# Joining a 64-bit weight's sign and low bits by half-word passes in an attention and gated feed-forward kernel

## The chip, the cores and the metric

The kernel runs on one core of one Trainium2 chip, as one program. The metric is device microseconds of one execution. Each number of the result is a median over runs, with the lowest and highest beside it. The engines have short names: PE multiplies matrices, DVE works on vectors, ACT applies functions and scales, POOL works across partitions and issues some DMAs, SP issues most DMAs. ACT issues DMAs too, the weight loads among them.

## The reference

Attention over 8 batches of 8 heads, 576 positions, head size 64, with a causal mask and a bias from a running sum of `s`; then, for the 4608 tokens of width 512, a gated layer of width 1536.

```python
scores = scale * np.matmul(q, k.transpose(0, 1, 3, 2))
s_pos = np.maximum(s, 0.0)
cum = np.cumsum(s_pos, axis=-1)
bias = -(cum[:, :, :, None] - cum[:, :, None, :])
scores = np.where(causal, -1000000000.0, scores + np.minimum(bias, 0.0))
scores = scores - np.max(scores, axis=-1, keepdims=True)
attn = np.exp(scores)
attn = attn / (np.sum(attn, axis=-1, keepdims=True) + 1e-09)
attn_out = np.matmul(attn, v)
x = attn_out.transpose(0, 2, 1, 3).reshape(B * S, H * D)
gate = 1.0 / (1.0 + np.exp(-(x @ w_gate)))
val = x @ w_val
out = (gate * val @ w_out).astype(np.float32)
```

`q`, `k`, `v` and `s` come in 32-bit floats. The three weight matrices come in 64-bit floats, and the kernel turns them into 32-bit floats itself.

## The kernel before

**Heads.** Attention goes head by head, each in five tiles of query rows (64 rows, then four of 128). The program is written as a sequence of ticks, five to a head. The first 8 heads (one batch) run in 32-bit floats: scores on PE (`n_s`, L575), masked and reduced to a row minimum of the negated scores on DVE (`n_max`, L584), the exponential on ACT (L587), a transpose on PE (L596) copied out by ACT (L597), the product with `v` on PE (`n_av`, L605). A score bank is given back to PE when DVE has reduced it. Later heads use high and low 16-bit parts and transposing DMAs (`s_part`, `max_part` with L471, `p_part`, `av_part`).

**Weights.** They come in 18 steps (`wsteps`): 12 for the columns of `w_gate` and `w_val`, 128 at a time, and 6 for the rows of `w_out`, 256 at a time. A step holds 1024 weights in each of the 128 partitions. `load_weight` (L253 to L260) brings them as pairs of 32-bit words, low word first, into a raw buffer: `ws`, parts of `w2all`, or parts of `t2f`. `decode_weight` makes a 32-bit float from each pair in the buffer `a` (the names `wa`, or a part of `w2all`). `split_weight` sums the squares on ACT (L287), adds them up across the partitions on POOL (L289), makes a power-of-two scale on DVE (L125, L127), and writes a high and a low 16-bit part (ACT L292, DVE L293). The raw buffers are few, so the load of a later step waits until an earlier one has been decoded.

**The decode.** A 64-bit float has its sign, an 11-bit exponent and the first 20 bits of the fraction in the high word. ACT (L272) reads the high word as a 32-bit float and multiplies it by 2^-112, which shifts the exponent's range so that 3 bits to the left it is that of a 32-bit float. Then three DVE passes work on the result: L273 shifts left by 3 and clears the sign into a buffer `m`, L274 puts the sign bit back from `a`, and L275 adds the three top bits of the low word, shifted right by 29. L273 has one tensor operand, L274 and L275 have two.

**Order.** Engines run their own lists in order. The lists are made when the kernel is built, by a scheduler that follows the written order, priorities (`first`) and its own estimate of time; so a change to one pass can change the order of instructions on every engine. Up to tick 44 the weight steps are called at fixed ticks, later a few ahead of the feed-forward units that use them. Feed-forward units (`ffn_in` with L657, `ffn_out` with L687) begin at tick 44 and fill PE between attention pieces.

Of the kernel before, what the change touches and what calls it, by code (L numbers as in the profile page):

```python
# [7 lines left out]
F16 = mybir.dt.float16  # L8
F32 = mybir.dt.float32
F32R = mybir.dt.float32r  # L10
I32 = mybir.dt.int32
I64 = mybir.dt.int64
AF = mybir.ActivationFunctionType
ALU = mybir.AluOpType
# [9 lines left out]
def tile_attention_then_gated_ffn(  # L24
# [11 lines left out]
    nc = tc.nc  # L36
# [33 lines left out]
    w1 = [cp.tile([P, NC, 2, 2, P], F16, name=f"w1_{f}") for f in range(NF)]  # L70

    w2all = cp.tile([P, NF // 2, 2, 8, 2, DM // 8], F16, name="w2all")
# [49 lines left out]
    def pow2_of(dst, ss, tag):  # L122

        e = wp.tile([P, 1], I32, tag="xe", name=f"xe_{tag}")
        nc.vector.tensor_scalar(e, ss.bitcast(I32), 1, 0x3F800000, ALU.logical_shift_right, ALU.bitwise_and)  # L125
        n = dst.shape[1]
        nc.vector.tensor_scalar(dst.bitcast(I32), e.to_broadcast([P, n]) if n > 1 else e, -1.0, 204.0 * 2.0 ** 23,  # L127
                                ALU.mult, ALU.add)

    def inverse_pow2(dst, sc):  # L130
        nc.vector.tensor_scalar(dst.bitcast(I32), sc.bitcast(I32), -1.0, 254.0 * 2.0 ** 23, ALU.mult, ALU.add)

# [79 lines left out]

    raw0 = lp.tile([P, 8 * P, 2], I32, name="ws0")
    dec0 = lp.tile([P, 8 * P], I32, name="wa0")
    flat = w2all.rearrange("p f l h x n -> p (f l h x n)").bitcast(I32)
# [11 lines left out]
    def room(n):  # L227

        o, f = wsteps[n]
        if o == 0:  # L230
            return raw[f % 3], dec[f % 3], n - 3
        i, j, last = outroom[f // 2]
        return raw[i], dec[j], last
# [30 lines left out]
    def decode_weight(n):  # L264

        o, f = wsteps[n]
        r, a, _ = room(n)
        if not wide:
            return a.bitcast(F32)
        m = w2all[:, f // 2].rearrange("p l h x n -> p (l h x n)") if o else w1[f].rearrange("p c g l n -> p (c g l n)")  # L270
        m = m.bitcast(I32)
        nc.scalar.activation(a.bitcast(F32), r[:, :, 1].bitcast(F32), AF.Copy, scale=2.0 ** -112)  # L272
        nc.vector.tensor_scalar(m, a, 3, 0x7FFFFFF8, ALU.logical_shift_left, ALU.bitwise_and)  # L273
        nc.vector.scalar_tensor_tensor(a, a, -0x80000000, m, ALU.bitwise_and, ALU.bitwise_or)  # L274
        nc.vector.scalar_tensor_tensor(a, r[:, :, 0], 29, a, ALU.logical_shift_right, ALU.bitwise_or)  # L275
        return a.bitcast(F32)

    def split_weight(n, a):
# [41 lines left out]
    def weight_step():  # L320
        n = wnext["step"]
        while n and wnext["load"] < len(wsteps) and room(wnext["load"])[2] < n:
            if not NF <= wnext["load"] < NF + 2:
                load_weight(wnext["load"])
            wnext["load"] += 1
        split_weight(n, decode_weight(n))
        wnext["step"] = n + 1
# [413 lines left out]
    for n in range(nticks + 12):  # L741
# [13 lines left out]
        if 2 <= n < nticks + 2:  # L755
            a, z = divmod(n - 2, NTL)
# [5 lines left out]
        if 1 <= n < nticks + 1:  # L762
            a, z = divmod(n - 1, NTL)
# [7 lines left out]
        if 3 <= n < 3 + NTL * NN:  # L771
            with first():
                a, z = divmod(n - 3, NTL)
# [11 lines left out]
        if i < NH:  # L785
            p, j = divmod(i, 2)
            b, h = divmod(i, H)
# [79 lines left out]
            elif b == 1:  # L867
                if VSQ <= n < VSQ + vch:
                    v_square(2, n - VSQ)
                if VSQ + 5 <= n < VSQ + 5 + vch:  # L870
                    c = VSQ + 4 + vch - n
# [15 lines left out]
        if n >= NE and state["u"] < 2 * NF:  # L887
            fdone = min(NF, int((n - NE + 1) * FPT))
            while state["u"] < 2 * fdone:
                f = state["u"]  # L890
# [17 lines left out]
        m = n - (11 if n > 2 * NTL * H + 30 else 7)  # L908
        b = m // (NTL * H) if m >= 0 else 0
        if b >= 1:  # L910
            r = m - b * NTL * H + 1
# [39 lines left out]
```

## Time and profile before

| what | value |
|---|---|
| median of 3 runs | 1152.38 us (1151.87 to 1155.03) |
| profiled execution, span from first to last instruction | 1146.4 us |
| what lies around the span, by that median | 6.0 us |
| mean granted TensorE clock | 0.985 of full speed |
| PE, DVE, ACT, POOL busy, share of the span | 95%, 68%, 65%, 23% |
| DMA queue of SP and ACT (q1), share of 16 engines | 57.6% |
| first feed-forward matrix product (L657) | 119.2 us |
| decode passes on DVE, first and last start | 11.5 us and 175.2 us |

The profiled execution's own time outside its span is not listed, so the 6.0 us is the difference of the median and the span. Busy shares are averages over stages with different limits: an engine that is at 68% of the whole may be full in one stage. Where a row names a line, the tile names follow as output, arrow, inputs, with buffer numbers left out; a wait is given with the engine and line whose end came last.

### The profile page before, as it was taken

How to read it: one execution, taken by the hardware profiler on the slowest of the kernel's cores; microseconds unless marked ns; L12 is line 12 of the kernel's file. 1: busy time of each engine (PE TensorE's matmuls, PEld its weight loads, DVE VectorE, ACT ScalarE, POOL GpSimd, SP SyncE). 2: the span in 40 equal slices, each digit the busy share in tenths (PEclk: the TensorE clock that was granted, in tenths of full speed). 3: DMA queues.
4: the chain of work that ended last, by engine and by line, in shares of the span. 5: the costliest groups of instructions: out<-in, count | busy, mean ns of one | idle time of the engine just before them, and what ended most of it. 6: DMA issues, size and time to landing. Idle time of an engine off the chain costs nothing.

```text
span 1146.4 us, 30336 instructions
## 1 busy us (share of the span) xinstructions
PE 1091.6 (95%) x11644; PEld 853.5 (74%) x11644; DVE 776.1 (68%) x2395; ACT 749.5 (65%) x1465; POOL 261.3 (23%) x568
## 2 busy tenths in 40 slices
PE   6787888989999999999999999999999999999998
PEld 4566676658767887788777777778877887787775
DVE  6899999866787777776565677777777775222222
ACT  6989778667777777676665577767776764233222
POOL 6634233222232222121211122212222221000000
PEclk9889899999999999999999999999999999999999
DMA  9676868995989888777646498868887774000000
GB/s 280 201 217 161 185 139 181 183 189 130 171 164 175 164 178 167 141 150 138 145 79 139 89 178 166 166 144 171 156 161 138 150 124 88 13 20 20 1 19 19
DMA packets 445518, 157.62 MB, mean 137 GB/s; under 512 B 403583, under 2 KB 435839, under 8 KB 445374
## 3 DMA queue, kind: packets, MB, share of 16 engines
q1 hardware_dynamic: 418686, 127.38, 57.6%
q10 hardware_dynamic: 23328, 17.04, 4.9%
q0 software_dynamic: 3360, 11.27, 3.0%
q8 instruction: 91, 1.49, 0.5%
q14 instruction: 53, 0.43, 0.1%
HBM read 56.92 MB, written 9.58 MB: 58 GB/s over the span
## 4 chain that ended last, share of the span: by engine, by line
PE 76%; DMA 7%; DVE 5%; issue 5%; ACT 5%; SPq 1%; POOL 1%; ACTq 0%; DVEq 0%; POOLq 0%
PE gv L657 42%; PE o L687 22%; PE s L447 3%; PE s L446 3%; DMA qk<-in_q_dram 1%; PE av L506 1%; PE av L508 1%; PE av L507 1%; DMA v<-in_v_dram 1%; DVE e L471 1%; PE s L575 1%; DMA pt<-p 1%; DMA T<-T 1%; PE na_ps L605 1%; DMA nqk<-in_q_dram 1%
## 5 line engine op out<-in xcount | busy, mean ns | idle before, releaser
L657 PE MATMUL gv<-x,w 128*128 128x256 f16 (+3 forms) x6912 | 613.2, 246 | 5.3 <-DVE t2f L664 2.7
L657 PEld LDWEIGHTS <-w 128*128 128x128 f16 x6912 | 533.8, 98 | 61.5 <-issue 5.2
L687 PE MATMUL o<-w2all,h 128*128 128x512 f16 x1296 | 314.8, 379 | 0.0
L461 POOL TENSOR_SCALAR_AFFINE_SELECT rl<-rl 128x64 f32<-128x64 f32 (+1 forms) x280 | 111.5, 399 | 519.7 <-DVE em L471 465.3
L474 ACT ACTIVATE e<-e,em 128x576 f32<-128x576 f32 x280 | 154.6, 554 | 92.3 <-DVE em L471 90.2
L687 PEld LDWEIGHTS <-h 128*128 128x128 f16 x1296 | 123.6, 98 | 108.7 <-issue 2.4
L662 ACT ACTIVATE th<-gv,scb 128x256 f32<-128x256 f32 (+3 forms) x288 | 111.4, 412 | 139.3 <-PE gv L657 138.4
L664 DVE SCALAR_TENSOR_TENSOR t<-th,gv 128x256 f32<-128x256 f32 x192 | 80.2, 417 | 133.5 <-ACT th L662 132.5
L471 DVE CUSTOM_DVE_ANT_0 e<-s,rl,qkcf 128x288 f32<-128x288 f32 x280 | 135.8, 485 | 30.5 <-PE s L447 24.9
L672 ACT ACTIVATE h<-t,hsc 128x256 f16<-128x256 f32 x192 | 96.6, 503 | 80.0 <-DVE t L664 80.0
L483 DVE SCALAR_TENSOR_TENSOR p<-e,p 128x384 f16<-128x384 f32 x224 | 102.0, 495 | 40.2 <-ACT p L478 39.4
L673 DVE SCALAR_TENSOR_TENSOR h<-t,hsc,h 128x256 f16<-128x256 f32 x192 | 93.2, 486 | 43.3 <-ACT h L672 42.8
L478 ACT ACTIVATE p<-e 128x1152 f16<-128x1152 f32 x112 | 112.1, 1001 | 2.8
L506 PE MATMUL av<-v,pt 128*128 128x65 f16 x560 | 68.0, 193 | 6.9 <-DMA pt<-p 6.9
L507 PE MATMUL av<-v,pt 128*128 128x64 f16 x560 | 68.0, 192 | 0.0
L446 PE MATMUL s<-T 128*128 128x288 f16 (+2 forms) x246 | 64.6, 280 | 3.6 <-DMA T<-qk 2.6
L508 PE MATMUL av<-v,pt 128*128 128x65 f16 x560 | 67.9, 194 | 0.0
L447 PE MATMUL s<-T 128*128 128x288 f16 (+2 forms) x246 | 62.2, 282 | 2.4 <-DMA T<-T 2.4
L506 PEld LDWEIGHTS <-pt 128*128 128x128 f16 x560 | 52.4, 97 | 13.6 <-DMA pt<-p 8.8
L706 POOL DMA_DIRECT2D out_dram<-osb x34 | 19.4, 570 | 174.6 <-ACT osb L705 173.8
L409 POOL PARTITION_BROADCAST cr<-cr x63 | 57.5, 913 | 6.1 <-DVE em L584 5.7
L455 DVE TENSOR_SCALAR rl<-cr,qkcf 128x576 f32<-128x576 f32 x56 | 29.1, 520 | 40.1 <-POOL cr L409 39.9
(157 smaller groups left out, 1436.9 us busy)
## 6 DMA issues: line engine op xcount, KB each, us to landing
v<-v SPq DMA_DIRECT2D x56, 162.5 KB
out_dram<-osb POOLq DMA_DIRECT2D x34, 256.0 KB, 2.9
v<-in_v_dram SPq DMA_DIRECT2D x64, 128.0 KB
T<-T SPq DMA_DIRECT2D x82, 72.0 KB
t2f<-in_v_dram SPq DMA_DIRECT2D x20, 288.0 KB
qk<-in_q_dram SPq DMA_DIRECT2D x17, 288.0 KB
qk<-in_k_dram SPq DMA_DIRECT2D x17, 288.0 KB
w2all<-in_moe_w_gate_dram ACTq DMA_DIRECT2D x7, 512.0 KB
```

The lines of the kernel that those rows point to most:

```text
L446: nc.tensor.matmul(ps[:, : b_ - a], lhs, T[i][:, 0, a:b_], start=True, stop=False)
L447: nc.tensor.matmul(ps[:, : b_ - a], lhs, T[i][:, 2, a:b_], start=False, stop=True)
L461: nc.gpsimd.affine_select(rl[i][:, q0:w], rl[i][:, q0:w], pattern=[[-1, m]], compare_op=ALU.is_ge, fill=-MASKED if i < NN else MASKED, bas ...
L471: nc.vector.tensor_tensor_reduce(e_t[t][:, a:b_], ps[:, : b_ - a], rl[i][:, a:b_], c, init, ALU.add, ALU.min, acc)
L474: nc.scalar.activation(e_t[t][:, :w], e_t[t][:, :w], AF.Exp, bias=init, scale=-1.0)
L478: nc.scalar.activation(p_s[h_][:, 0], e_s[h_], AF.Copy, scale=PSCALE)
L483: nc.vector.scalar_tensor_tensor(flat[:, LOW[t] * P : (LOW[t] + t) * P], e_t[t][:, : t * P], PSCALE, flat[:, kb * P : (kb + t) * P], ALU.m ...
L506: nc.tensor.matmul(AV[i][:, t], hi, v_[:, D : 2 * D + 1], start=kb == 0, stop=False)
L657: nc.tensor.matmul(ps[:, gv, a:e], w1[f][:, cc, gv, wl], x_of(b, cc)[:, xl, c0 + a : c0 + e], start=(c == 0), stop=(c == 3 * NC - 1))
L662: nc.scalar.activation(th[:, a:e], ps[:, 0, a:e], AF.Tanh, scale=scb[b][:, f : f + 1])
L672: nc.scalar.activation(h[:, 0], t2, AF.Copy, scale=hsc[:, f : f + 1])
L687: nc.tensor.matmul(ps[:m], h[:, hl, tt * P : tt * P + m], w2[f][:, wl], start=(f == 0 and c == 0), stop=(f == NF - 1 and c == 2))
```

## The change

The decode keeps ACT's scaling and has one merging pass instead of two. Two passes with one operand work on the loaded words as 16-bit halves (half 0 and 1 are the low word, 2 and 3 the high word). The first puts the top three bits of half 1 into half 0; the second puts the sign bit of half 3 into half 1. The low word then holds the sign at its top, the three bits at its bottom and zeros between. The one merging pass shifts ACT's result left by 3, which drops its sign, and joins it with that word. The buffer `m` isn't used any more.

```diff
+I16 = mybir.dt.int16
...
         if not wide:
             return a.bitcast(F32)
-        m = w2all[:, f // 2].rearrange("p l h x n -> p (l h x n)") if o else w1[f].rearrange("p c g l n -> p (c g l n)")
-        m = m.bitcast(I32)
+        half = r.bitcast(I16)
+        nc.vector.tensor_scalar(half[:, :, 0], half[:, :, 1], 13, 7, ALU.logical_shift_right, ALU.bitwise_and)
+        nc.vector.tensor_scalar(half[:, :, 1], half[:, :, 3], -0x8000, None, ALU.bitwise_and)
         nc.scalar.activation(a.bitcast(F32), r[:, :, 1].bitcast(F32), AF.Copy, scale=2.0 ** -112)
-        nc.vector.tensor_scalar(m, a, 3, 0x7FFFFFF8, ALU.logical_shift_left, ALU.bitwise_and)
-        nc.vector.scalar_tensor_tensor(a, a, -0x80000000, m, ALU.bitwise_and, ALU.bitwise_or)
-        nc.vector.scalar_tensor_tensor(a, r[:, :, 0], 29, a, ALU.logical_shift_right, ALU.bitwise_or)
+        nc.vector.scalar_tensor_tensor(a, a, 3, r[:, :, 0], ALU.logical_shift_left, ALU.bitwise_or)
         return a.bitcast(F32)
```

In the changed kernel the two half passes are L272 and L273, ACT's scaling is L274 and the merging pass L275; other lines near them move by one. The number of instructions on DVE stays the same.

DVE's list at the first weight step, in the first head, before. In a row stand line, operation, output, arrow, inputs and size; in brackets are the engines or DMA queues whose end it awaits. ISA is the row minimum, whose name `em` carries the tile and the piece; the last number is only the buffer's.

```order
L584 ISA e_80,em_4_1_226<-s_4_288_184,cr_147,em_4_0_224 128x288 [waits DVE_49,PE_49,Pool_49]
L584 ISA em_4_1_226 128x1
L273 TENSOR_SCALAR w_0_66<-wa_137 128x1024 [waits Activation_49]
L274 SCALAR_TENSOR_TENSOR wa_137<-wa_137,w_0_66 128x1024 [waits DVE_49]
L584 ISA e_80,em_3_0_254<-s_3_0_219,cr_147 128x448 [waits PE_49,Pool_49]
L584 ISA em_3_0_254 128x1
L275 SCALAR_TENSOR_TENSOR wa_137<-ws_136,wa_137 128x1024 [waits DMAHW6_49,DMAHW5_49,DVE_49]
L584 ISA e_79,em_2_0_275<-s_2_0_244,cr_147 128x320 [waits PE_49,Pool_49]
```

And the same place in the changed kernel:

```order
L272 TENSOR_SCALAR ws_136<-ws_136 128x1024 [waits DMAHW6_49,DMAHW5_49]
L584 ISA e_80,em_4_1_226<-s_4_288_184,cr_147,em_4_0_224 128x288 [waits DVE_49,PE_49,Pool_49]
L584 ISA em_4_1_226 128x1
L273 TENSOR_SCALAR ws_136<-ws_136 128x1024 [waits DVE_49]
L275 SCALAR_TENSOR_TENSOR wa_137<-wa_137,ws_136 128x1024 [waits DVE_49,Activation_49]
L584 ISA e_80,em_3_0_254<-s_3_0_219,cr_147 128x448 [waits PE_49,Pool_49]
L584 ISA em_3_0_254 128x1
L272 TENSOR_SCALAR w2all<-w2all 128x1024 [waits DMAHW7_49,DMAHW1_49]
L584 ISA e_79,em_2_0_275<-s_2_0_244,cr_147 128x320 [waits PE_49,Pool_49]
```

The first half pass moved ahead of a row minimum and awaits the load itself; only the merging pass still awaits ACT, and the second step's first half pass stands a row minimum earlier than its L273 did.

DVE's list between the fourth head and the fifth, where the weight steps 5 to 7 stand before:

```order
L273 TENSOR_SCALAR w_6_72<-wa_137 128x1024
L275 SCALAR_TENSOR_TENSOR w2all<-w2all 128x1024
L615 TENSOR_TENSOR nx_638<-na_ps_562,ner_635 128x5x64
L632 SCALAR_TENSOR_TENSOR x_130<-nx_ps_3_524,vsc_327,x_130 128x256
L274 SCALAR_TENSOR_TENSOR wa_137<-wa_137,w_6_72 128x1024
L273 TENSOR_SCALAR w_7_73<-w2all 128x1024
L175 TENSOR_REDUCE vso_1003<-vst_1001 128x1
L275 SCALAR_TENSOR_TENSOR wa_137<-ws_136,wa_137 128x1024
L274 SCALAR_TENSOR_TENSOR w2all<-w2all,w_7_73 128x1024
L125 TENSOR_SCALAR xe_v_1007<-vso_1003 128x1
L125 TENSOR_SCALAR xe_w_1063<-wtot_1061 128x1
L584 ISA e_80,em_4_0_737<-s_4_0_711,cr_586 128x288
```

And the same place in the changed kernel:

```order
L275 SCALAR_TENSOR_TENSOR wa_137<-wa_137,ws_136 128x1024
L612 RECIPROCAL ner_635<-ner_635 128x5
L615 TENSOR_TENSOR nx_638<-na_ps_562,ner_635 128x5x64
L275 SCALAR_TENSOR_TENSOR w2all<-w2all 128x1024
L272 TENSOR_SCALAR w2all<-w2all 128x1024
L273 TENSOR_SCALAR w2all<-w2all 128x1024
L272 TENSOR_SCALAR ws_136<-ws_136 128x1024
L273 TENSOR_SCALAR ws_136<-ws_136 128x1024
L176 TENSOR_REDUCE vso_1003<-vst_1001 128x1
L584 ISA e_80,em_4_0_737<-s_4_0_711,cr_586 128x288
```

Ahead of the row minimum `em_4_0` of the next head stood four merging passes and two one-operand passes; now it is two merging passes, of steps 6 and 7, and four half passes that belong to steps 8 and 9 already, whose merging passes stand behind that minimum.

## The prediction

> **What bounds the kernel now.** First the span cut into stages, in the windows view. Each row is a stretch in us, its length, each engine's busy time, the granted TensorE clock, the share of the DMA engines and GB/s.
>
> ```profile
> core 0 of [0], span 1146.4 us
> core 0: us, PE busy (x) PEld busy (x) DVE busy (x) ACT busy (x) POOL busy (x), PEclk, DMA share, GB/s
> 10.00:60.00 50.00, 37.26 (x224) 28.12 (x223) 41.29 (x101) 46.29 (x91) 29.66 (x46) 0.88 0.82 236
> 60.00:120.00 60.00, 50.15 (x288) 39.89 (x287) 52.86 (x137) 51.18 (x95) 22.98 (x37) 0.84 0.70 188
> 120.00:180.00 60.00, 48.84 (x519) 40.54 (x517) 55.74 (x160) 45.39 (x78) 20.23 (x36) 0.97 0.84 172
> 180.00:240.00 60.00, 55.64 (x562) 42.04 (x561) 49.74 (x177) 47.92 (x95) 17.76 (x37) 1.00 0.94 179
> 240.00:1147.00 907.00, 895.26 (x10045) 699.61 (x10043) 571.02 (x1809) 555.05 (x1103) 164.34 (x385) 1.00 0.62 123
> ```
>
> From 240 us on PE is busy 895.26 of 907 us: the matrix work bounds that stretch, and nothing on DVE can shorten it. What can be won lies ahead of it. PE stands idle 12.7 us in 10 to 60 (50 less 37.26), 9.9 in 60 to 120, 11.2 in 120 to 180 and 4.4 in 180 to 240. Whatever is cut there moves the full stretch forward and shortens the run by as much. Who keeps PE waiting differs: in 10 to 60 ACT is the fullest engine (46.29 of 50, DVE 41.29), in 60 to 120 the two are level, in 120 to 180 DVE is fullest (55.74 of 60, ACT 45.39).
>
> Next the view of waits from 10 to 180 us: engine and line that waited, whom for, total us, times, the longest.
>
> ```profile
> PEld s L575 <- DVE em L584: 12.1, 14, 1.9
> ...
> PE s L575 <- DVE em L584: 7.7, 10, 1.5
> ...
> ACT w2all L287 <- DVE wa L275: 3.2, 2, 2.1
> ```
>
> PE's largest wait here is for the row minimum on DVE (L584), which frees a score bank. It is late because DVE works in order and weight passes stand ahead of it, as DVE's timeline shows:
>
> ```profile
> 74.10 1.21 DVE L274 SCALAR_TENSOR_TENSOR wa<-wa,w 128x1024 int32<-128x1024 int32 x1
> 75.23 0.68 DVE L273 TENSOR_SCALAR w<-w2all 128x1024 int32<-128x1024 int32 x1
> 75.83 0.34 DVE L584 CUSTOM_DVE_ANT_0 e<-s,cr 128x192 f32<-128x192 f32 x1
> 76.11 0.08 DVE L584 DVE_READ_ACCUMULATOR2_ANT em<- 128x1 f32 x1
> 76.11 1.21 DVE L275 SCALAR_TENSOR_TENSOR w2all<-w2all 128x1024 int32<-128x1024 int32 x1
> 77.25 1.25 DVE L275 SCALAR_TENSOR_TENSOR wa<-ws,wa 128x1024 int32<-128x1024 int32 x1
> 78.42 1.21 DVE L274 SCALAR_TENSOR_TENSOR w2all<-w2all,w 128x1024 int32<-128x1024 int32 x1
> 79.56 0.21 DVE L584 CUSTOM_DVE_ANT_0 e<-s,cr 64x64 f32<-64x64 f32 x1
> ```
>
> Between the minimum at 75.83 and the next at 79.56 stand three merging passes, 3.5 us in which PE gets no bank back. So a shorter decode does pay, though not at its full length in every stage.
>
> **The change, part by part.** The groups of DVE instructions by line and form: busy us, mean ns of one, idle before.
>
> ```profile
> L274 DVE SCALAR_TENSOR_TENSOR w2all<-w2all,w 128x1024 int32<-128x1024 int32 x8 | 10.2, 1272 | 0.0
> L275 DVE SCALAR_TENSOR_TENSOR w2all<-w2all 128x1024 int32<-128x1024 int32 x8 | 10.2, 1270 | 0.0
> ...
> L275 DVE SCALAR_TENSOR_TENSOR wa<-ws,wa 128x1024 int32<-128x1024 int32 x6 | 7.4, 1226 | 0.0
> ...
> L274 DVE SCALAR_TENSOR_TENSOR wa<-wa,w2all 128x1024 int32<-128x1024 int32 x6 | 7.3, 1212 | 0.0
> ...
> L273 DVE TENSOR_SCALAR w<-w2all 128x1024 int32<-128x1024 int32 x8 | 5.5, 693 | 2.2 <-ACT w2all L272 2.2
> ...
> L274 DVE SCALAR_TENSOR_TENSOR wa<-wa,w 128x1024 int32<-128x1024 int32 x4 | 4.9, 1217 | 0.0
> ...
> L273 DVE TENSOR_SCALAR w2all<-wa 128x1024 int32<-128x1024 int32 x6 | 4.2, 702 | 0.0
> ...
> L273 DVE TENSOR_SCALAR w<-wa 128x1024 int32<-128x1024 int32 x4 | 2.7, 680 | 0.6 <-ACT wa L272 0.5
> L125 DVE TENSOR_SCALAR xe_w<-wtot 128x1 int32<-128x1 int32 x18 | 2.6, 146 | 6.4 <-POOL wtot L289 6.3
> ...
> L141 DVE TENSOR_TENSOR_SCAN cum<-sp_sb,zero 64x576 f32<-64x576 f32 x1 | 1.3, 1349 | 0.0
> ```
>
> Removed: 18 merging passes (L274) of 1.24 us (10.2, 7.3 and 4.9 make 22.4 us, by 18) and 18 one-operand passes (L273) of 0.69 us. Added: two one-operand passes of 1024 elements for each of the 18 steps. What stays: ACT's scaling, the last merging pass, and the split into high and low parts.
>
> The **unknown** is the duration of an added pass. It reads and writes 16-bit halves, one element every 8 bytes, in place; the trace has no such instruction. The low end is L273, a one-operand pass of the same 1024 elements over 32-bit words without gaps: 0.69 us. An upper end, should such a pass go one element at a time like a merging pass, is 1.24 us. The far end is the slowest rate per element on DVE, the scan: 1349 ns less the 146 ns of an instruction with next to no elements, over 576, is 2.09 ns each, so 2.28 us for 1024 elements. I take 0.69 us. It is the nearest row, the same operation on the same count with one source and one destination in SBUF. And L275 already reads one word every 8 bytes of the loaded pairs (wa<-ws,wa, 1226 ns) at the price of L274, which reads none with gaps (1212 and 1217 ns): that gap costs a read nothing. No row shows a gapped write.
>
> [...]
>
> **The sum.** A step changes on DVE by two times 0.69 less 0.69 less 1.24, that is by -0.55 us; 18 steps by -10.0 us. Where the passes lie, in the windows view of L273 alone:
>
> ```profile
> 10.00:60.00 50.00, 5.54 (x8) 0.88 0.82 236
> 60.00:120.00 60.00, 4.19 (x6) 0.84 0.70 188
> 120.00:180.00 60.00, 2.75 (x4) 0.97 0.84 172
> ```
>
> By stage, and these fractions are my choice: in 120 to 180 DVE is the fullest engine, so 4 times 0.55 counts whole, 2.2 us. In 60 to 120 ACT is as full, so half of 6 times 0.55, 1.65 us. In 10 to 60 ACT's work covers most of it, so a quarter of 8 times 0.55, 1.1 us. Together **4.95 us**. If ACT's cover were gone, all 10.0 us would come; if it held everywhere, only the 2.2.
>
> The moved parts I cost at nothing in the sum, and at some 3 us either way in the range. The half passes no longer wait for ACT: they read the loaded words and stand in DVE's queue where the load is awaited, as the rows of the order show, so the chain behind ACT shrinks from three DVE passes to one. That takes from the 3.2 us that ACT waited for L275. The price is that DVE itself now waits for the loads, with row minima queued behind it. ACT did so in the run before:
>
> ```profile
> L272 ACT ACTIVATE w2all<-w2all 128x1024 f32<-128x1024 f32 x8 | 9.3, 1164 | 1.7 <-DMA w2all<-in_moe_w_val_dram 1.6
> ...
> L272 ACT ACTIVATE wa<-ws 128x1024 f32<-128x1024 f32 x6 | 6.9, 1145 | 1.8 <-DMA ws<-in_moe_w_val_dram 1.8
> ```
>
> The two come to 3.4 us, about what the shorter chain gives. On POOL and SP nothing is added; their weight sums and loads only follow the steps, and POOL is busy 20 to 30 us of each stretch before 180. A raw buffer is still freed by the last merging pass, so the loads are bound as before.
>
> The profiled execution has a span of 1146.4 us, and 1152.38, the median of the runs, lies 6.0 us above it; I carry those 6.0 us unchanged. 1146.4 less 4.95 is a span of 1141.5, and the time **1147.4 us**, 0.4% faster. About 0.3%, 3.5 us, is what a measurement of this kernel can tell from no change.
>
> **The rivals.**
> - *ACT and the new order eat the gain.* For it: ACT is busy 46.29 of 50 us in the first stretch, and holds the same passes as before; the loads now stop DVE. Against: DVE's 55.74 of 60 later on. Then 2.2 us, less up to 3.4 for loads, remain: between 1150.2 and 1153.6, middle 1152.
> - *One element at a time.* The half passes take 1.24 us, the change doesn't do what it says, since a shorter pass is paid twice: a step costs DVE 0.55 us more, and with the same fractions the run takes 1157.3. It decides from a pass of 0.965 us on, where two of them equal the 0.69 and 1.24 us removed. For it: 16-bit elements with gaps occur in no row; against: L273's rate on 32-bit ones.
> - *Gapped writes stall.* At the scan's rate two passes and a merge are 5.80 us where 3.17 stood, 18 times 2.63 is 47 us on DVE. Its idle time from 10 to 180 us is 20.1 us; if half of that takes some of it, 37 us are left, 1189. Same place and point of decision. [...]
>
> **How the numbers follow.** Forecast (0.69 us passes, about half of it gained) 0.43; ACT and order eat it 0.25; one element at a time 0.19; stalled writes 0.13. The forecast's own range is 1142.4 (all 10.0 us) to 1150.2. Faster by over 0.3%, below 1148.9, holds 0.41 of the forecast and 0.02 of the next: 0.43. Slower, above 1155.8, holds 0.15 of the third case, all of the fourth and 0.01 of the second: 0.29. The rest, 0.28, lies within. The range runs from 1141 to 1164: it takes in the first three cases with some 3 us for the order on each side, and leaves out most of the fourth.
>
> **What would show it.** The whole span's busy times, from the page:
>
> ```profile
> PE 1091.6 (95%) x11644; PEld 853.5 (74%) x11644; DVE 776.1 (68%) x2395; ACT 749.5 (65%) x1465; POOL 261.3 (23%) x568
> ```
>
> In the groups by line, L272 and L273 of the changed kernel at 0.69 us (step right), 1.24 (second rival) or near 2.3 (third). DVE's total should be about 10 us below 776.1, ACT's unchanged. In the windows, PE's idle time from 10 to 180 us down from 33.8 by some 5, and the stretch of full PE starting that much earlier. In the waits, L575 for L584 shorter than 7.7 us; a new wait of DVE for the weight loads would speak for the first rival. Wrong it would be if the DVE time falls and PE's idle time doesn't.

## The result and the profile after

| kernel | median us (lowest to highest) | runs |
|---|---|---|
| before | 1153.12 (1151.87 to 1155.03) | 4 |
| changed | 1186.41 (1184.95 to 1189.09) | 4 |

The changed kernel takes 1.0289 times the time of before, interval 1.027 to 1.0309: **33 us slower**, where 1147.4 us was forecast, outside the range of 1141 to 1164.

First the changed kernel's page: span, busy times by engine, and the granted TensorE clock in 40 slices.

```profile
span 1183.2 us, 30344 instructions
...
PE 1103.6 (93%) x11644; PEld 861.0 (73%) x11644; DVE 787.9 (67%) x2395; ACT 751.2 (63%) x1465; POOL 270.1 (23%) x568
...
PEclk8968789899999999999999999999999999999999
```

The span is 36.8 us longer than the 1146.4 of before. DVE is 11.8 us busier (787.9 against 776.1), where some 10 us less were forecast. PE runs the same 11644 products but is busy 12.0 us longer (1103.6 against 1091.6), and it stands idle 79.6 us of the span where it was 54.8. The 36.8 us are these two: 24.8 us more idle PE, 12.0 us more time in the same products. (By the medians it is 33.3 us: the profiled run of the changed kernel, at 1184.95 us, lies 1.75 us above its span, that of before was a quick one. So of the 6.0 us that the prediction carried around the span, some 4 were the spread between runs.)

The windows view of the changed kernel, in the same stretches; columns as before.

```profile
10.00:60.00 50.00, 36.90 (x212) 27.62 (x210) 42.78 (x94) 41.44 (x79) 30.83 (x40) 0.90 0.76 221
60.00:120.00 60.00, 37.07 (x201) 29.37 (x201) 51.71 (x114) 46.41 (x86) 28.98 (x36) 0.75 0.63 179
120.00:180.00 60.00, 44.87 (x345) 35.05 (x346) 48.18 (x131) 42.96 (x74) 19.32 (x33) 0.80 0.66 131
180.00:240.00 60.00, 51.68 (x523) 40.85 (x521) 45.67 (x165) 41.71 (x84) 15.75 (x34) 0.94 0.95 173
240.00:1184.00 944.00, 928.73 (x10354) 724.75 (x10351) 594.14 (x1884) 574.98 (x1140) 168.84 (x400) 1.00 0.62 122
```

From 240 us on PE is full in both kernels (928.73 of 944 us here). The loss lies ahead: PE is idle 22.9 us in 60 to 120 (9.9 before), 15.1 in 120 to 180 (11.2 before), and runs 201 products there where 288 ran, 345 where 519 ran. The granted clock falls too: 0.75 for 0.84 in 60 to 120, 0.80 for 0.97 in 120 to 180. Ten us at a time, the changed kernel first:

```profile
60.00:70.00 10.00, 5.08 (x22) 4.53 (x23) 7.76 (x12) 8.80 (x20) 7.90 (x9) 0.50 0.70 226
70.00:80.00 10.00, 4.76 (x30) 3.80 (x29) 8.20 (x21) 4.72 (x7) 0.60 (x2) 0.84 0.81 233
80.00:90.00 10.00, 5.31 (x16) 3.47 (x16) 9.29 (x22) 7.46 (x13) 6.16 (x8) 0.50 0.43 141
```

and the kernel before:

```profile
60.00:70.00 10.00, 10.00 (x42) 8.45 (x41) 8.36 (x21) 8.94 (x15) 3.23 (x4) 0.58 1.11 335
70.00:80.00 10.00, 7.53 (x53) 5.80 (x51) 10.00 (x21) 8.05 (x16) 4.08 (x6) 1.00 0.32 89
80.00:90.00 10.00, 7.36 (x38) 4.72 (x39) 8.13 (x29) 8.98 (x17) 3.29 (x9) 1.00 1.12 290
```

In 80 to 90 the changed kernel's PE has half its clock throughout and is busy for 5.31 us; before, it had the full clock and was busy for 7.36. No value below 0.50 stands in these rows, and a value between 0.50 and 1.00 is a mean of the two: the clock records in the traces of both kernels, and of e2 to e12 below, hold 1.00 and 0.50 alone. So the whole span's mean tells the time at half: 0.968 of 1183.2 us gives 2 times 0.032 times 1183.2, 76 us; before, 0.985 of 1146.4 gives 34 us. All runs bear out the direction, at a smaller distance: 0.960 to 0.968 in the four of the changed kernel, 0.973 to 0.985 in the seven of before that stood beside e11 and e12. The profiled run of before is at the top of its kind: the 26 runs of before beside e7 to e10 have a median clock of 0.979, which by the same sum is some 48 us at half.

The groups of DVE instructions by line and form, changed kernel: busy us, mean ns of one, idle time before and its releaser.

```profile
L273 DVE TENSOR_SCALAR w2all<-w2all 128x1024 int16<-128x1024 int16 x9 | 12.5, 1392 | 0.0
L272 DVE TENSOR_SCALAR w2all<-w2all 128x1024 int16<-128x1024 int16 x9 | 12.2, 1355 | 4.5 <-DMA w2all<-in_moe_w_val_dram 2.9 <-DMA w2all<-in_moe_w_out_dram 1.6
...
L272 DVE TENSOR_SCALAR ws<-ws 128x1024 int16<-128x1024 int16 x6 | 8.3, 1389 | 1.4 <-DMA ws<-in_moe_w_val_dram 1.4
...
L273 DVE TENSOR_SCALAR t2f<-t2f 128x1024 int16<-128x1024 int16 x3 | 4.4, 1479 | 0.0
...
L272 DVE TENSOR_SCALAR t2f<-t2f 128x1024 int16<-128x1024 int16 x3 | 4.0, 1325 | 4.3 <-DMA t2f<-in_moe_w_out_dram 4.3
```

A half pass takes 1.33 to 1.48 us by these means, not 0.69, and DVE now stands still for weight loads: 4.5, 1.4 and 4.3 make 10.2 us, where before it never did. The waits from 10 to 180 us:

```profile
PEld s L575 <- DVE em L584: 26.4, 15, 3.1
...
PE s L575 <- DVE em L584: 23.1, 14, 2.9
...
ACT e L587 <- DVE em L584: 10.3, 9, 3.6
```

PE's wait for the row minimum has grown from 7.7 to 23.1 us, its weight loads' from 12.1 to 26.4 (the two lie largely in the same gaps). DVE's timeline shows one place (start us, duration, instruction, in brackets the idle time before):

```profile
72.73 1.30 DVE L272 TENSOR_SCALAR ws<-ws 128x1024 int16<-128x1024 int16 x1 [1.18 <-DMA ws<-in_moe_w_val_dram]
74.06 1.30 DVE L273 TENSOR_SCALAR ws<-ws 128x1024 int16<-128x1024 int16 x1
75.16 0.20 DVE L176 TENSOR_REDUCE vso<-vst 128x1 f32<-128x4 f32 x1
75.20 0.45 DVE L584 CUSTOM_DVE_ANT_0 e<-s,cr 128x288 f32<-128x288 f32 x1
```

Row minima follow in DVE's list behind 1.18 us of waiting for a load and 2.6 us of half passes. Here the wait and the longer pass stand ahead of the same consumer.

### The profile page after: what moved, and what is told of

It is laid out like the page before. It is cut to its first block, busy times and chain, and to the rows that moved or that the text cites. A ratio compares the mean times of both kernels' runs of the same rounds, so it can differ in the third digit from the quotient of the medians.

```text
span 1183.2 us, 30344 instructions
## 1 busy us (share of the span) xinstructions
PE 1103.6 (93%) x11644; PEld 861.0 (73%) x11644; DVE 787.9 (67%) x2395; ACT 751.2 (63%) x1465; POOL 270.1 (23%) x568
## 4 chain that ended last, share of the span: by engine, by line
PE 69%; DMA 4%; issue 4%; DVE 3%; POOL 1%; SPq 1%; ACT 1%; DVEq 0%; POOLq 0%; ACTq 0%
PE gv L657 39%; PE o L687 21%; PE s L447 2%; PE s L446 2%; DMA v<-in_v_dram 1%; PE av L506 1%; PE av L508 1%; DMA T<-qk 1%; PE av L507 1%; DMA pt<-p 1%; DVE e L471 1%; POOL rl L461 1%; PE av L510 1%; PE av L511 1%; DVE p L483 0%
## 5 line engine op out<-in xcount | busy, mean ns | idle before, releaser
L657 PE MATMUL gv<-x,w 128*128 128x256 f16 (+3 forms) x6912 | 620.3, 247 | 4.3 <-ACT x L631 2.2
L575 PE MATMUL s<-nk,nq 128*128 128x288 f32 (+4 forms) x96 | 38.8, 507 | 23.3 <-DVE em L584 23.1
```

The costliest lines, as they stand in the source:

```text
L657: nc.tensor.matmul(ps[:, gv, a:e], w1[f][:, cc, gv, wl], x_of(b, cc)[:, xl, c0 + a : c0 + e], start=(c == 0), stop=(c == 3 * NC - 1))
```

## The experiments

Two theories stood after the result. **A, slow writes:** what costs is the duration of the half passes; with passes of 0.69 us the forecast would come. **B, the place:** the passes stand ahead of ACT's scaling and wait for loads in DVE's list, or any new list costs; short passes would not help much. All ratios are to the kernel before, run on the same chip; "us above" is the ratio less one, times 1152 us.

### e1: the passes by themselves

Eight instructions of each form, on loaded data, on an otherwise quiet DVE; attention and the feed-forward layer are left out.

> Only DVE passes over 1024 elements, eight of each form, one after the other, nothing of the reference. [...] Rival 'other engines slow the passes (POOL or ACT on the same buffers)': all forms with one operand take about 0.69 us here. [...]

The groups by line; `raw` and `oth` hold pairs of 32-bit words (a step of 8 bytes from one used element to the next), `den` is dense.

```profile
L53 DVE TENSOR_SCALAR oth<-raw 128x1024 int16<-128x1024 int16 x8 | 10.4, 1296 | 0.0
L50 DVE TENSOR_SCALAR raw<-raw 128x1024 int16<-128x1024 int16 x8 | 9.3, 1343 | 0.0
L47 DVE TENSOR_SCALAR raw<-raw 128x1024 int16<-128x1024 int16 x8 | 9.2, 1338 | 0.0
L59 DVE TENSOR_SCALAR raw<-den 128x1024 int16<-128x1024 int16 x8 | 9.2, 1335 | 0.0
...
L56 DVE TENSOR_SCALAR den<-raw 128x1024 int16<-128x1024 int16 x8 | 5.8, 726 | 0.0
...
L35 DVE TENSOR_SCALAR den<-den 128x1024 int32<-128x1024 int32 x8 | 5.5, 694 | 1.2 <-DMA den<-in_moe_w_gate_dram 0.9
L68 DVE TENSOR_SCALAR raw<-raw 128x512 int16<-128x512 int16 x8 | 5.1, 747 | 0.0
L65 DVE TENSOR_SCALAR den<-den 128x1024 int16<-128x1024 int16 x8 | 5.0, 719 | 0.0
L41 DVE TENSOR_SCALAR den<-raw 128x1024 int32<-128x1024 int32 x8 | 4.9, 688 | 0.0
L44 DVE TENSOR_SCALAR raw<-den 128x1024 int32<-128x1024 int32 x8 | 4.9, 688 | 0.0
```

L47 and L50 are the two half passes: 1338 and 1343 ns, about as long as in the changed kernel, so it isn't the other engines' work that makes them long. L59 reads dense and writes 16 bits every 8 bytes: 1335. L56 turns that round, reads every 8 bytes and writes dense: 726. So the **write** sets the time, and L53, which writes into another buffer, shows that it isn't the work in place (1296). L44 writes whole 32-bit words every 8 bytes: 688, like the dense 694. L65 writes 16 bits every 4 bytes in place: 719. Of these forms with one operand only the 16-bit write with an 8-byte step is slow (1296 to 1343 ns). Between 512 and 1024 elements (L68 and L47, 747 and 1338 ns) it adds 1.15 ns an element.

### e2 and e3: short passes, and a long pass in the kernel before

e2 is the changed kernel with 32-bit passes into the dense buffer `m`, still ahead of ACT; the sign is left out. e3 is the kernel before with its first pass as a two-operand one, which gives other weights.

```diff
 e2
-half[:, :, 0] <- (half[:, :, 1] >> 13) & 7;  half[:, :, 1] <- half[:, :, 3] & -0x8000
+m <- (r[:, :, 0] >> 29) & 7;  m <- m & 7
-a <- (a << 3) | r[:, :, 0]
+a <- (a << 3) | m
 e3
-nc.vector.tensor_scalar(m, a, 3, 0x7FFFFFF8, SHL, AND)
+nc.vector.scalar_tensor_tensor(m, a, 3, r[:, :, 0], SHL, AND)
```

> The changed decode with its two half passes replaced by a 32-bit pass that reads every other word and writes a dense buffer, and a dense 32-bit pass in place; the sign bit is left out. Number of DVE instructions as in the change. [...] Rival 'the new order (DVE waits for the loads, row minima behind it) is the cause': the passes are short but the run stays above 1170 us. [...]

> The kernel before with its one-operand first pass (0.69 us) turned into a two-operand pass of 1.24 us; the decoded weights lose their fraction bits through it. That is +0.55 us on DVE in each of 18 steps, 10 us in all, near the 11.8 us by which DVE's busy time rose with the change, while ACT still stands ahead of all DVE passes. Theory 'DVE time alone': the run gets slower by about the 33 us of the change, or at least 20. Rival 'most of the loss comes from order and load waits': it gets slower by 3 to 12 us.

e2: 1162.69 us, 1.0082 (1.0052 to 1.0112). e3: 1168.97 us, 1.0142 (1.0112 to 1.0172). Theory A alone falls: with short passes and 7 us less DVE work (769.1 us) than before, e2 is still 9 us slower. And e3 loses 16 us for 11.5 us more on DVE, with nothing put ahead of ACT. That lies between the two ranges expected for e3, and e2 stays below the 1170 us that its rival, the new order, was to exceed.

### e4 and e5: the same lists, shorter passes

Here the changed kernel's two passes become 32-bit ones on the same buffer, both (e4, the sign left out) or the first alone (e5). The lists of all engines are the changed kernel's, row for row, so only durations differ.

```diff
 e4 and e5
-nc.vector.tensor_scalar(half[:, :, 0], half[:, :, 1], 13, 7, SHR, AND)
+nc.vector.tensor_scalar(r[:, :, 0], r[:, :, 0], 29, 7, SHR, AND)
 e4 alone
-nc.vector.tensor_scalar(half[:, :, 1], half[:, :, 3], -0x8000, None, AND)
+nc.vector.tensor_scalar(r[:, :, 0], r[:, :, 0], 7, None, AND)
```

> The changed kernel with every engine's list of instructions unchanged, row for row, but both half passes done over 32-bit words, one word every 8 bytes, in place (shown alone at 0.695 us, against 1.34 us for the 16-bit form). The sign bit is left out. DVE gets 18 times 2 times 0.65, that is 23 us, shorter than in the change. Theory 'duration of the 16-bit writes': the run comes down by most of those 23 us or more, to 1145 to 1165. Rival 'the new order': it stays above 1175, since DVE still stands ahead of the loads and the row minima behind it. Second rival 'the clock': the time follows the sum of stretches at half TensorE clock (34 us in the kernel before, 75 us in the change); it should come near 1150 only if these come near 34 us.

> The same with the first half pass alone done over 32-bit words; the second stays in 16 bits. All lists unchanged. The lowest three bits come from the low word whole, so the values stay right to those bits. DVE is 11.7 us shorter than in the change. Theory 'duration of the 16-bit writes': about half way between the change (1186) and the run with both short. Rival 'the new order': no step.

e4: 1172.42 us, 1.0176 (1.0137 to 1.0215). e5: 1176.37 us, 1.021 (1.0167 to 1.0254). Short passes bring back 13 of the 33 us (by the ratios), one of them alone some 9, though the intervals of e4 and e5 overlap; 20 us stay. So e4 lies between what the two theories expected. The page and the waits (10 to 180 us) of e4:

```profile
PE 1107.1 (95%) x11644; PEld 863.8 (74%) x11644; DVE 769.6 (66%) x2395; ACT 750.1 (64%) x1465; POOL 259.7 (22%) x568
```

```profile
DVE t2f L272 <- DMA t2f<-in_moe_w_out_dram: 8.0, 3, 4.0
...
PE s L575 <- DVE em L584: 7.1, 9, 2.3
...
DVE w2all L272 <- DMA w2all<-in_moe_w_val_dram: 3.3, 2, 3.1
```

DVE is 18.3 us less busy than in the changed kernel (769.6 against 787.9), and PE's wait for the row minimum is back at 7.1 us, where before it was 7.7. So in these lists the long passes are what tripled that wait. DVE's waits for weight loads did not go with it: they are longer in e4, 14.1 us in all against 10.2, and yet PE waits for the row minimum no longer than before. What e4 still loses is elsewhere: of its span's 24.2 us above 1146.4, 15.5 are PE busy time (1107.1 against 1091.6), and its mean clock is 0.967, as low as in the change.

### e6 and e7: what the writes go to, and who waits for ACT

e6 keeps the 16-bit passes ahead of ACT but writes into the dense `m`, 4 bytes apart. e7 puts ACT first, takes the sign from ACT's result in a 32-bit pass, writes the low bits into `m`, and has one merge: the change's instruction counts, short passes, and every pass behind ACT.

```diff
 e6 (q is m as pairs of 16-bit halves)
+q[:, :, 0] <- (half[:, :, 1] >> 13) & 7;  q[:, :, 1] <- half[:, :, 3] & -0x8000
 nc.scalar.activation(a, r[:, :, 1], Copy, scale=2.0 ** -112)
 e7 (m16 is m as pairs of 16-bit halves)
 nc.scalar.activation(a, r[:, :, 1], Copy, scale=2.0 ** -112)
+m <- a & 0x80000000;  m16[:, :, 0] <- (half[:, :, 1] >> 13) & 7
+a <- (a << 3) | m
```

> The changed decode, whole, but with the half passes writing into the dense buffer that the kernel before used between its passes: the 16-bit writes are then 4 bytes apart, not 8 (alone: reads 8 bytes apart and dense 16-bit writes took 0.73 us, reads and writes 4 bytes apart 0.72). Instructions get a new order. Theory 'the 8-byte step of the 16-bit write is what costs': the passes take 0.69 to 0.75 us and DVE's busy time is 8 to 12 us below that of the kernel before. Time: by the forecast's sum 1147; by the rival that the order and the clock decide, as in the run with a dense 32-bit target (1162.7), 1155 to 1170.

> A whole decode with one merging pass that waits for ACT as the kernel before did: the sign goes by a 32-bit pass from ACT's result into the dense buffer, then the three low bits by a 16-bit pass into the same buffer (writes 4 bytes apart), then the one merge. Per step 0.69 + 0.73 + 1.22 = 2.64 us on DVE against 3.17 before, 9.5 us less in all, and no wait of DVE for a weight load ahead of ACT. Theory 'standing ahead of ACT is what costs once the passes are short': 1143 to 1153. Rival 'any new order of the lists costs some 10 to 20 us by more half-clock time': 1158 to 1172, with over 60 us at half clock and no load waits on DVE.

e6: 1170.11 us, 1.0149 (1.0112 to 1.0186). DVE's busy time in e6 is 772.0 us, 4 below before, where 8 to 12 were expected. e7: 1155.72 us, 1.0032 (1.0019 to 1.0045), the best of all the versions and still not faster than before; it lies between the two ranges that were expected. Its short passes take 771 and 770 ns in the largest groups, up to about a tenth longer than such forms in e1 (694 to 726):

```profile
L275 DVE TENSOR_SCALAR w<-w2all 128x1024 int16<-128x1024 int16 x8 | 6.2, 771 | 0.0
L274 DVE TENSOR_SCALAR w<-w2all 128x1024 int32<-128x1024 int32 x8 | 6.2, 770 | 4.4 <-ACT w2all L273 4.4
```

DVE waits for ACT here (4.4 us in this group), never for a weight load.

### e8 to e10: a shorter pass, and lists that merely differ

e8 is the kernel before with its first merge as a one-operand pass (the form of L273, 0.69 us there; the sign is left out). e9 and e10 are controls: the kernel before plus one extra pass of 8 elements, in weight step 3 or 9. They do the same work, but the scheduler makes other lists.

```diff
 e8
-nc.vector.scalar_tensor_tensor(a, a, -0x80000000, m, AND, OR)
+nc.vector.tensor_scalar(a, m, 0x7FFFFFF8, None, AND)
 e9 (e10: n == 9), after L273
+n == 3 and nc.vector.tensor_scalar(m[:, :8], a[:, :8], 3, 0x7FFFFFF8, SHL, AND)
```

> The kernel before with its first merging pass (1.24 us) turned into a one-operand pass in place (0.69 us); the sign is left out. Same dependencies as before, DVE 10 us shorter, new lists. Theory 'short decode helps if it waits for ACT': 1143 to 1152 (the forecast's sum, in the kernel before). Rival 'any new order costs': 1158 to 1172.

> The kernel before with one more tiny pass (8 elements, under 0.2 us) in the decode of weight step 3, on values that it doesn't change. The work is the same but for that; the scheduler makes other lists (the order of PE, DVE, ACT differs in many places). Theory 'the decode's own duration and waits set the time': within 3 us of the kernel before. Rival 'any new order of the lists costs': 1158 to 1172, with the time at half clock up from 34 us to 60 or more.

> The same control with the tiny pass in weight step 9: a second new order with the same work. Theory: within 3 us of the kernel before. Rival: 1158 to 1172 again; if the two controls differ by more than 5 us, the order alone spreads the time that much.

e8: 1158.34 us, 1.0055 (1.0029 to 1.0082). e9: 1158.42 us, 1.0047 (1.0016 to 1.0078). e10: 1156.7 us, 1.0054 (1.0029 to 1.0079). In both controls, lists that only differ cost 5 to 6 us by the ratios, 2 to 9 by the intervals; neither is within the 3 us of one theory, and only e9 reaches the 1158 of the other. Taking 7 us off DVE's busy time (e8) shows no gain either. e8's ten runs spread from 1152.77 us at a mean clock of 0.979 to 1166.89 at 0.969, and between these the time follows the clock (correlation -0.93): one program with one set of lists, and the granted clock goes with 14 us of its time. Elsewhere the tie is looser: -0.65 in the ten runs of e10, whose slowest, 1164.16 us, had a clock of 0.979, and -0.39 in the 26 runs of before.

### e11 and e12: the two factors crossed

e11 has the change's slow passes behind ACT (they write into the high word, which ACT must have read first). e12 is e7 with one operand changed, so that both short passes can stand ahead of ACT.

```diff
 e11, behind the activation
+half[:, :, 3] <- half[:, :, 3] & -0x8000;  half[:, :, 2] <- (half[:, :, 1] >> 13) & 7
+a <- (a << 3) | r[:, :, 1]
 e12, against e7
-nc.vector.tensor_scalar(m, a, -0x80000000, None, AND)
+nc.vector.tensor_scalar(m, r[:, :, 1], -0x80000000, None, AND)
```

> A whole decode with the change's 16-bit passes (writes 8 bytes apart, 1.33 us each), but put into the high word, which ACT reads: so both passes must wait until ACT has read it, as the passes of the kernel before waited. One merging pass. Theory 'two separate costs': the slow writes cost here what they cost ahead of ACT (14 us between the change and the run with the same order and short passes), on top of the 4 to 6 us of any new order: 1166 to 1176, no load waits on DVE. Rival 'the slow writes cost only because they stand ahead of ACT': 1155 to 1162. Rival 'standing ahead of ACT costs nothing by itself': 1180 to 1190, as in the change.

> The twin of the run with the gated dense target (1155.7): the same three DVE passes at the same durations, but the first takes the sign from the loaded high word in place of ACT's result, so that both short passes may stand ahead of ACT and await the load themselves. Theory 'standing ahead of ACT costs': 1161 to 1172, with load waits on DVE of 4 us or more. Rival 'only the order's accident': within 3 us of its twin, 1153 to 1159.

e11: 1172.67 us, 1.0162 (1.014 to 1.0185). e12: 1167.33 us, 1.0121 (1.0103 to 1.0138). In us above before:

| | behind ACT | ahead of ACT |
|---|---|---|
| short passes | 3.7 (e7), 6.3 (e8) | 9.4 (e2), 13.9 (e12), 17.2 (e6), 20.3 (e4) |
| slow 16-bit writes | 18.7 (e11) | 33.3 (the change) |

Down a column, slow writes cost 15.0 us (e11 less e7) and 13.0 (the change less e4, with identical lists). Along a row, standing ahead of ACT costs 10.2 us (e12 less e7) and 14.6 (the change less e11). The widths of the ratios' intervals leave each difference some 2.5 to 5 us. So neither short passes nor the place behind ACT alone undoes the loss. Only the change and e4 have the same lists, though; every other pair also differs in its lists, and new lists alone cost 5 to 6 us. With e2 in place of e12 the place ahead of ACT would cost 5.7 us, hardly more than that. The sums come out about alike in both columns and both rows, but the time isn't lost in the same way:

| profiled run | PE busy, us | PE idle, us | DVE's waits for weight loads, 10 to 180 us |
|---|---|---|---|
| before | 1091.6 | 54.8 | 0 |
| e7, short, behind ACT | 1095.3 | 59.3 | 0 |
| e12, short, ahead | 1106.2 | 59.6 | 5.6 |
| e4, short, ahead | 1107.1 | 63.5 | 14.1 |
| e11, slow, behind | 1110.5 | 63.5 | 0 |
| the change, slow, ahead | 1103.6 | 79.6 | 10.2 |

Slow writes behind ACT cost mostly PE busy time (e11 against e7: 15.2 us busy, 4.2 idle); with the change's lists they cost idle time alone (16.1 us more idle than e4, 3.5 less busy). Of the runs in the table PE's wait for the row minimum tripled in the change alone (23.1 us, against 4.2 in e7, 10.2 in e12 and 7.1 in e4); e11, with passes as long (1.32 to 1.42 us), has it about as before:

```profile
PEld s L575 <- DVE em L584: 14.1, 12, 2.5
PE s L575 <- DVE em L584: 8.2, 7, 2.2
```

In e12 DVE waits for weight loads as was expected (4 us or more), but PE's idle time is that of e7, and what it loses is busy time. The clocks of e7, e12 and e11, in that order:

```profile
core 0: 1154.6 us, clock 0.982
```

```profile
core 0: 1165.8 us, clock 0.972
```

```profile
core 0: 1174.0 us, clock 0.964
```

By the sum used above these are 42, 65 and 85 us at half clock, and PE's busy time in the table, for the same products in each, goes along.

The traces also show what half clock follows. The clock changes in steps of 3.41 us. Cut into such steps, the first 250 us of the traces of both kernels and of e2 to e12 have 662 steps at full clock. In 79 of them PE was busy for less than half of the step, and in 76 of these cases the next step stood at half; of the 474 in which PE was busy for 0.7 or more, none was followed by half clock. The way back is harder: of 71 steps at half clock with PE busy for under 0.8 none was followed by full clock, of 169 above that 101 were. In the changed kernel, PE is busy 1.19 of the 3.41 us from 73.49 to 76.90 at full clock, and the next 3.41 us stand at 0.50. No long wait is needed: in 68 of the 76 cases no single gap of PE in or across the step reached 3.41 us. This is an order in time that all the traces share, not an experiment.

## Why the prediction was wrong, point by point

- **What bounds the kernel: right.** PE is full after 240 us (928.73 of 944 us), and every us of PE time lost ahead of it lengthens the run. PE's largest wait there is for the row minimum behind weight passes, and in the change it tripled; it took longer passes and their place ahead of ACT together, since neither e4 (7.1 us) nor e11 (8.2) shows it.
- **The added pass, "I take 0.69 us": the step that failed.** It is 1.33 to 1.48 us. The prediction said that "no row shows a gapped write" and let the rate of 32-bit words and the free gapped read stand for it. The read was right (726 ns), the 16-bit write was not (1335), while 16-bit writes 4 bytes apart (719) and 32-bit writes 8 bytes apart (688) are as short as the dense pass (694). With it a step costs DVE not 0.55 us less but 0.81 us more (two times 1.37 less 0.69 less 1.24). This term has the wrong sign, and it alone is 13 us of the loss with equal lists (the change against e4), 15 with others (e11 against e7). That the gapped read is free was read from L275, a pass of 1.2 us with two operands, which need not speak for a pass twice as fast: it came out so, but that row didn't show it.
- **The moved parts, "at nothing in the sum, and at some 3 us either way": failed too, and as much.** With passes near the forecast's (0.69 to 0.80 us) and the change's lists (e4) the run is 20 us slower than before, not 5 us faster. Of that, standing ahead of ACT is 10 to 15 us by the pairs of the table; over all the programs there it is less sure. A mechanism was named: "DVE itself now waits for the loads, with row minima queued behind it"; it was priced by ACT's 3.4 us of waiting, while DVE waits 10.2 us. But e4 has 14.1 us of these waits and no longer wait of PE for the row minimum than before, so this isn't shown to be the way in which the place costs. New lists of themselves cost 5 to 6 us (e9, e10), where the sum had nothing.
- **The fractions of the gain: failed in the other direction too.** DVE time saved brought about nothing: 7 us less in e7 and e8 leave both 4 to 6 us above before, at most 3 us better than the controls. DVE time added costs 0.7 to 1.4 us for each us: 13 us for 18.3 more (the change against e4), 16 for 11.5 (e3, new lists included).
- **The clock: not in the sum at all.** The windows shown before had clocks of 0.84 to 0.97 in the early stretches, and nothing was priced from them. A third of the loss of the profiled run (12.0 of 36.8 us) is PE busy longer for the same products, with 76 us at half clock where 34 were (some 48 in a typical run of before).
- **The rivals.** "One element at a time" had the pass nearly right (1.24 us, a merging pass's measured time; how many elements a pass takes at a time no run shows) and the time wrong (1157.3), since it used the same small fractions and no price for the place. "Gapped writes stall" came near the time (1189 against 1186.4) for a wrong reason: its pass was 2.28 us. "ACT and the new order eat the gain" had the wait for loads and the wrong size.

What stays open: how much of the 20 us is the place ahead of ACT and how much the particular lists. Four programs with short passes there lie 9 to 20 us above before (e2, e12, e6, e4), with 3.7, 5.6, 4.7 and 14.1 us of DVE waiting for weight loads, so these waits don't account for the loss and the list matters as much as the place. Why other lists for the same work cost 5 us wasn't found. That gaps of PE bring on the half clock is shown as an order in time only: no run made a gap on purpose.

## What to carry to other kernels

Time an instruction's exact form by itself, write step and element width included, before counting passes: here 16-bit halves cost twice what 32-bit words on the same places do (1335 and 688 ns in e1). A pass that no longer waits for another engine is not free of waiting (10.2 us for loads here): look at what it waits for now, and at what stands behind it in its engine's list. Look at the granted clock as well as at idle time: most of what e12 and e11 lose is the same matrix products taking longer (14.6 of 19.4 us of span, and 18.9 of 27.6). In a kernel whose lists come from a scheduler, an edit that changes next to nothing else cost 5 to 6 us twice here, so run such a control before a gain below that is believed.

## What the runs showed of the hardware that was not expected

- A 16-bit write with an 8-byte step takes 1296 to 1343 ns for 1024 elements per partition when DVE works alone (e1), 32-bit words written on the same step 688, and 16-bit elements with a 4-byte step 719.
- The same 11644 products keep PE busy from 1091.6 us (before) to 1110.5 us (e11), at mean clocks of 0.985 and 0.964; nearly all of the time at half clock lies ahead of 240 us, from where the mean clock is 1.00 to two places (before and the change to the end, e11 as far as 300 us).
- The clock changes between 1.00 and 0.50 in steps of 3.41 us. Half clock followed 76 of the 79 steps at full clock in which PE was busy for less than half, and none of the 474 in which it was busy for 0.7 or more, although only 8 of the 76 had a gap of 3.41 us.
